# Top-k attention and two MoE layers on one core: the first chunk's first two feature pairs multiplied with three quarters of x before the last quarter is there, and the first queries transposed in other PSUM banks

## The chip, the cores and the metric

The kernel runs on one core of a Trainium2 chip. The metric is the device time of one execution in microseconds (us), lower is better. Engines: PE is TensorE (matmuls, transposes), DVE is VectorE, ACT is ScalarE, POOL is GpSimd, SP is SyncE, which here issues all the DMAs. Every engine takes its instructions in the order that is fixed when the program is built.

## What is computed

```python
def _attn_ref(q, k, v):                       # (4, 8, 576, 64) each, top_k = 32
    scores = scale * np.matmul(q, k.transpose(0, 1, 3, 2))
    kth = np.partition(scores, -top_k, axis=-1)[..., -top_k:-top_k + 1]
    scores = np.where(scores >= kth, scores, -1000000000.0)
    attn = np.exp(scores - np.max(scores, axis=-1, keepdims=True))
    attn = attn / (np.sum(attn, axis=-1, keepdims=True) + 1e-09)
    return np.matmul(attn, v).astype(np.float32)

x = attn_out.transpose(0, 2, 1, 3).reshape(2304, 512)
x = ((1 / (1 + np.exp(-(x @ w_gate)))) * (x @ w_val)) @ w_out     # 512 -> 1536 -> 512
h = np.maximum(x @ w_in, 0.0)                                     # 512 -> 2048
return ((h * h) @ w_out2).astype(np.float32)                      # 2048 -> 512
```

The weights arrive as 64-bit numbers; everything else is 32-bit.

## The kernel before

The 2304 tokens are cut into 18 blocks of 128, and these into chunks: six chunks of one block, then six of two. For each chunk the attention goes through four pairs of heads (`hp` 0 to 3). Such a pair loads its queries and values (`Pair.load`), turns its queries with PE (`queries`, line 341, result `qpt`, copied by ACT to `qt`), makes scores for each head (`scores`, line 381, PSUM tile `sp`, copied by ACT to `S`), finds the 32 largest of each row with four MAX8 and three MATCH_REPLACE8 on DVE (`rank`, lines 392 and 393), applies the threshold and the exponential on ACT (lines 418 and 434), turns the probabilities with PE (`transpose`, lines 482 and 493, tiles `tp` and `tq`) and multiplies with the values (`values`, line 543, tile `xp`). ACT copies `xp` to one quarter of the chunk's x (line 551): head pair hp is quarter hp of the 512 features. In the first chunk the keys are also turned on the way (`prep_keys`, lines 167 to 175: `kpt` on PE, `kp` by ACT, `kl` by DVE).

The first two chunks (`PLAIN`, their x is the tile `x_plain`) go through the MoE in fp32 in `moe32`. Layer 1 has six feature pairs `fp`. A pair (`l1_pair`) is 16 matmuls into one PSUM bank `pg` of the pool `ps_w`: gate and value weights (`wg`, `wv`), two blocks of 128 features each, four quarters of x each (line 932; quarter c is the innermost loop). Then ACT takes the tanh of the gate half (line 941, `th`), POOL and DVE make `g`, and `l1_acc` (line 954) adds eight matmuls with `wo` into `acc`. After six pairs ACT copies `acc` back over x (line 972, "the x2 copy" below), and layer 2 follows (`l2_pair` with `wi` into `ph`, line 979; `l2_acc` with `w2`, line 996). Each fp32 matmul is two records in the trace.

Before that the weights must be made into fp32: blocks of 128 x 512 are fetched as raw 64-bit words (line 591, 512 KB each), and `conv` turns them with two ACT instructions a block (lines 613 and 620), one of DVE a pair of blocks (617) and one of POOL a block (621). `gram_pair` (line 639, tiles `wg_n`, `wv_n`, `wo_n`, ...) sums squares of the weights on PE for the scales of the later fp16 path. There are 68 blocks in the order wg, wv, wo, wi, w2. Chunks 3 to 12 then use weights split in two fp16 parts.

What sets the order: the loop at the end of the kernel calls `weight_step()`, the attention generator `att` and the `moe32` generator `body` by three clocks `tw`, `ta` and `tm`, and `at(t)` gives what it emits the priority t. A list scheduler then orders all instructions of each engine by priority and by its own estimates of when they can run. In this program it had already put single matmuls of `pg_0` and `pg_1` early: one each after the first, the second and the third quarter of x, since the first accumulation needs only `wg` and one quarter at a time. The PSUM pools have two banks each: `ps_t` (tag `tr`: all the transposes `kpt`, `qpt`, `tp`, `tq` and `xp`), `ps_a` (tag `acc`: the sums), `ps_w` (tag `wk`: `pg`, `ph`), and `ps_s` two more for the scores.

Of the kernel before, what the change touches and what calls it, by code (L numbers as in the profile page):

```python
# [10 lines left out]
F32 = mybir.dt.float32  # L11
# [10 lines left out]
P = 128  # L22
# [15 lines left out]
PLAIN = (0, 1)  # L38
# [26 lines left out]
DTURN = 5  # L65
DTAIL = 14
KA = 7
GLATE = 30.0
EARLY = ("wg", "wv")
PB = 10  # L70


TB = 15
# [3 lines left out]
def tile_topk_attention__then__two_moe_layers(  # L77
# [14 lines left out]
    nc = tc.nc  # L92
# [196 lines left out]
    class Pair:  # L289
# [9 lines left out]
        def load(self):  # L299
            ci, hp = self.ci, self.hp  # L300
            for tt in self.tts:
                qn = apool.tile([P, 2, 2, D], F32, tag="qn", bufs=2, name=f"qn_{tt}_{hp}")
                for b, s0, o, n in pieces(tt):
                    for a in range(2):
                        nc.sync.dma_start(
                            qn[o : o + n, :, a, :],
                            q[b, 2 * hp : 2 * hp + 2, s0 : s0 + n].rearrange("h p d -> p h d"),
                        )
                self.qt[tt] = qn
            for b, _, _ in self.segs:  # L310
                if ci >= TCI:
                    t = apool.tile(
                        [P, 2, 2, CB + 1, D], F16, tag="v", bufs=2, name=f"v_{ci}_{hp}_{b}"
                    )
                    nc.sync.dma_start(t, vscr[(b, hp)])
                    self.vt[b] = t
                    continue
                t = apool.tile([P, 2 * CB + 1, D], F32, tag="v", bufs=2, name=f"v_{ci}_{hp}_{b}")
                src = v[b, 2 * hp : 2 * hp + 2]
                for j in range(2):  # L320
                    nc.sync.dma_start(
                        t[:, j * CB : (j + 1) * CB], src[j, 0:SM].rearrange("(p c) d -> p c d", c=CB)
                    )
                    nc.sync.dma_start(t[j * ST : (j + 1) * ST, 2 * CB], src[j, SM:S])
                self.vt[b] = t
# [10 lines left out]
        def queries(self, tts):  # L336
            for tt in tts:
                qn = self.qt[tt]
                pt = ps_t.tile([P, 512], F32, tag="tr", name=f"qpt_{tt}_{self.hp}")
                for j in range(2):  # L340
                    nc.tensor.transpose(  # L341
                        pt[:, j * P : (j + 1) * P], qn[:, j].rearrange("p a d -> p (a d)"), ident
                    )
                p3 = pt[:, 0 : 2 * P].rearrange("p (j t) -> p j t", j=2)
                ps = pieces(tt)
                for b, _, o, n in ps:

                    qt = apool.tile([P, 2, 2, P], F32R, tag="qt", bufs=2, name=f"qt_{tt}_{self.hp}_{b}")
                    for p_b, _, o_, n_ in ps:
                        if p_b != b:  # L350
                            nc.gpsimd.memset(qt.bitcast(F32)[:, :, :, o_ : o_ + n_], 0.0)
                    sl = slice(o, o + n)
                    nc.scalar.copy(qt[:, 0, :, sl], p3[:, :, sl])

                    whole = qn.rearrange("p j a d -> p j (a d)")[:, :, sl]
                    nc.scalar.copy(whole, p3[:, :, sl])
                    nc.gpsimd.tensor_tensor(
                        qt[:, 1, :, sl], whole, qt[:, 0, :, sl], op=ALU.subtract
                    )
                    self.qt[(tt, b)] = qt  # L360
# [108 lines left out]
        def transpose(self, j, i, wk, dg):  # L469
# [4 lines left out]
                    [P, CB, self.N], F32, tag="PT", bufs=3, name=f"PT_{self.ci}_{h}"  # L474
                )
            ptr = self.pt[j]
            tp = ps_t.tile([P, 512], F32, tag="tr", name=f"tp_{tt}_{h}")
            for c in range(CB):
                o, x = tp[:, c * P : (c + 1) * P], wk[:, c * P : (c + 1) * P]
                if self.ci < DIAG:  # L480
# [441 lines left out]
    def moe32(ci, xt):  # L922
# [1 line left out]
        assert N == P  # L924
        accs = []

        def l1_pair(fp):
            pg = ps_w.tile([P, 512], F32, tag="wk", name=f"pg_{ci}_{fp}")
            for t, name in enumerate(("wg", "wv")):
                for e in range(2):  # L930
                    for c in range(KM):
                        nc.tensor.matmul(
                            pg[:, (2 * t + e) * N : (2 * t + e + 1) * N],
                            fblk(name, c, (2 * fp + e) * P, P),
                            xt[:, c, :],
                            start=(t == 0 and e == 0 and c == 0),
                            stop=(c == KM - 1),
                            skip_group_check=True,
                        )
            th = mpool.tile([P, 2 * N], F32, tag="hi", bufs=HIB, name=f"th_{ci}_{fp}")  # L940
            nc.scalar.activation(th, pg[:, 0 : 2 * N], AF.Tanh, scale=0.5)
            nc.gpsimd.tensor_scalar(th, th, 1.0, 0.5, op0=ALU.add, op1=ALU.mult)
# [4 lines left out]
        def l1_acc(fp, g):  # L947
# [3 lines left out]
            for e in range(2):  # L951
                f = 2 * fp + e
                for d in range(KM):
# [6 lines left out]
                        skip_group_check=True,  # L960
                    )

        prev = None
        for fp in range(NF1 // 2):
            g = l1_pair(fp)
# [55 lines left out]

    nchunk = len(chunks)
    done = set()
    xsp = {}

    xts = {}
# [4 lines left out]
    def attention():  # L1031
# [62 lines left out]
        def tail(n, after=None):  # L1094
# [30 lines left out]
            if j == 1 and i == len(pr.tts) - 1:  # L1125
                if pr.ci < TCI:
                    pr.values()
                if pr.hp == NHP - 1:
                    if pr.ci in PLAIN:
                        xsp[pr.ci] = pr.xt  # L1130
# [106 lines left out]
    def at(t):  # L1237
        tc.cur_priority = base + int(t * 50)
# [19 lines left out]
    for ci in PLAIN:  # L1258
        n = 0
        while True:  # L1260
            if nstep[0] == len(steps):
                tw = 1e8
            if body is None and ci in xsp:
                have("wv")
                body = moe32(ci, xsp.pop(ci))
                tm = max(ta, tw if tw < 1e8 else 0)
            if body is not None and tm <= min(tw, ta):
                if n == 1:
# [85 lines left out]
```

## Time and profile before

| | |
|---|---|
| median of 3 runs | 1227.74 us (1220.72 to 2309.37) |
| the profiled execution | 1218.28 us, of which the span from first to last instruction is 1216.2 us |
| busy in the span | PE 1158.1 us, DVE 919.5, POOL 833.4, ACT 802.0 |
| granted TensorE clock, mean of the span | 0.989 |
| DMA | 153.91 MB, 127 GB/s over the span; 350 GB/s and more between 30 and 90 us |

Times in rows are microseconds from the span's start. A timeline row gives the start, the length from the first start to the last end, the instruction, how many of them, and in brackets how long the engine stood idle before it and what released it. The granted clock is the share of full speed that the throttle let PE have in a stretch: its two levels are 1.2 and 2.4 GHz, so 0.50 is a stretch wholly at the lower one. Matmuls overlap: the step from one group's start to the next group's start tells what a group costs.

### The profile page before, as it was taken

How to read it: one execution, taken by the hardware profiler on the slowest of the kernel's cores; microseconds unless marked ns; L12 is line 12 of the kernel's file. 1: busy time of each engine (PE TensorE's matmuls, PEld its weight loads, DVE VectorE, ACT ScalarE, POOL GpSimd, SP SyncE). 2: the span in 40 equal slices, each digit the busy share in tenths (PEclk: the TensorE clock that was granted, in tenths of full speed). 3: DMA queues.
4: the chain of work that ended last, by engine and by line, in shares of the span. 5: the costliest groups of instructions: out<-in, count | busy, mean ns of one | idle time of the engine just before them, and what ended most of it. 6: DMA issues, size and time to landing. Idle time of an engine off the chain costs nothing.

```text
span 1216.2 us, 30575 instructions
## 1 busy us (share of the span) xinstructions
PE 1158.1 (95%) x11477; PEld 941.4 (77%) x11477; DVE 919.5 (76%) x1921; ACT 802.0 (66%) x1695; POOL 833.4 (69%) x1294
## 2 busy tenths in 40 slices
PE   6879999999799799999999999999999999999998
PEld 5659878878679678788787688768876886886875
DVE  5899878899779988999999799999699969010010
ACT  3999985777767777777778667766577666222122
POOL 1698984687875688878879967896597659324223
PEclk9889999999899999999999999999999999999999
DMA  6999963324353477666676666556245513200000
GB/s 153 355 359 320 305 181 105 89 68 133 99 148 104 116 153 156 143 138 135 144 173 136 137 146 130 122 117 145 50 89 126 99 40 63 45 1 1 18 1 18
DMA packets 243187, 153.91 MB, mean 127 GB/s; under 512 B 193120, under 2 KB 209504, under 8 KB 243040
## 3 DMA queue, kind: packets, MB, share of 16 engines
q1 hardware_dynamic: 243040, 151.97, 49.3%
q8 instruction: 90, 1.47, 0.5%
q14 instruction: 57, 0.47, 0.1%
HBM read 105.51 MB, written 18.09 MB: 102 GB/s over the span
## 4 chain that ended last, share of the span: by engine, by line
PE 48%; DVE 2%; DMA 1%; SPq 0%; issue 0%; ACT 0%; POOL 0%; DVEq 0%; POOLq 0%
PE acc L899 10%; PE ph L878 10%; PE acc L813 7%; PE pv L773 7%; PE pg L773 7%; PE sp L381 3%; PE xp L516 3%; DVE mx L392 1%; DVE W L393 1%; PE qpt L341 1%; DMA kn<-in_k_dram 1%; DMA PT<-pp 0%; PE kpt L167 0%; PE x2pq L845 0%; DVE x2s L848 0%
## 5 line engine op out<-in xcount | busy, mean ns | idle before, releaser
L392 DVE MAX8 mx<-W 128x8 f32<-128x576 f32 x432 | 327.7, 759 | 10.9
L393 DVE MATCH_REPLACE8 W<-mx,W 128x576 f32<-128x576 f32 x288 | 213.9, 743 | 0.0
L878 PE MATMUL ph<-x,wi_w 128*128 128x256 f16 (+1 forms) x1920 | 191.8, 252 | 4.4 <-ACT r L887 2.8
L899 PE MATMUL acc<-w_w,rh 128*128 128x512 f16 x768 | 182.2, 379 | 1.6 <-POOL rh L891 1.6
L878 PEld LDWEIGHTS <-wi_w 128*128 128x128 f16 x1920 | 155.9, 98 | 30.7 <-issue 4.7
L773 PE MATMUL pg<-xs,wg_w 128*128 128x256 f16 (+1 forms) x1440 | 145.4, 251 | 1.3 <-ACT th L783 1.3
L773 PE MATMUL pv<-xs,wv_w 128*128 128x256 f16 (+1 forms) x1440 | 142.6, 251 | 2.1 <-DVE x2s L848 1.7
L381 PE MATMUL sp<-kst,qt 128*128 128x288 f32 x608 | 132.9, 328 | 9.4 <-DMA kst<-ks 4.7
L464 POOL TENSOR_TENSOR pp<-S,pp 128x512 f16<-128x512 f32 x192 | 137.1, 736 | 1.9
L773 PEld LDWEIGHTS <-wg_w 128*128 128x128 f16 x1440 | 117.2, 98 | 19.1 <-issue 3.4
L418 ACT ACTIVATE S<-S,mx 128x576 f32<-128x576 f32 x144 | 111.8, 776 | 27.7 <-DVE mx L392 27.3
L813 PEld LDWEIGHTS <-wo_w 128*128 128x128 f16 x1440 | 118.7, 99 | 13.9 <-issue 2.4
L899 PEld LDWEIGHTS <-rh 128*128 128x128 f16 x768 | 72.1, 98 | 73.4 <-POOL rh L891 1.8
L773 PEld LDWEIGHTS <-wv_w 128*128 128x128 f16 x1440 | 117.0, 98 | 15.4 <-issue 2.7
L392 DVE MAX8 mx<-S 128x8 f32<-128x576 f32 x144 | 107.2, 745 | 26.6 <-ACT S L384 26.4
L384 ACT COPY S<-sp 128x576 f32<-128x576 f32 x144 | 91.8, 637 | 50.6 <-PE sp L381 44.9
L785 DVE TENSOR_TENSOR th<-pv,th 128x512 f32<-128x512 f32 (+1 forms) x60 | 34.6, 576 | 119.2 <-PE pv L773 118.5
L462 POOL TENSOR_SCALAR S<-S,bs 128x576 f32<-128x576 f32 x96 | 71.9, 749 | 54.4 <-ACT pp L461 53.7
L393 DVE MATCH_REPLACE8 W<-mx,S 128x576 f32<-128x576 f32 x144 | 106.9, 743 | 0.0
L813 PE MATMUL acc<-gh,wo_w 128*128 128x256 f16 (+1 forms) x1104 | 104.9, 249 | 1.9 <-ACT gh L788 1.9
L381 PEld LDWEIGHTS sp<-kst,qt 128*128 128x128 f32 x608 | 90.2, 191 | 18.9 <-DMA kst<-ks 5.0
L890 POOL TENSOR_TENSOR r<-r 128x512 f32<-128x512 f32 (+1 forms) x80 | 69.5, 871 | 48.5 <-ACT rh L889 47.4
(236 smaller groups left out, 2222.2 us busy)
## 6 DMA issues: line engine op xcount, KB each, us to landing
kst<-ks SPq DMA_DIRECT2D x112, 288.0 KB, 3.1
v<-vd SPq DMA_DIRECT2D x32, 320.0 KB, 3.5
qn<-in_q_dram SPq DMA_DIRECT2D x128, 64.0 KB, 2.5
wi_r<-in_moe_w_in_dram SPq DMA_DIRECT2D x16, 512.0 KB, 6.4
w_r<-in_moe_w_out_dram SPq DMA_DIRECT2D x16, 512.0 KB, 4.9
v<-in_v_dram SPq DMA_DIRECT2D x56, 128.0 KB, 2.4
wg_r<-in_moe_w_gate_dram SPq DMA_DIRECT2D x12, 512.0 KB, 6.1
wv_r<-in_moe_w_val_dram SPq DMA_DIRECT2D x12, 512.0 KB, 7.3
```

Of the source, the lines that this page charges most:

```text
L381: nc.tensor.matmul(sp[:, e, 0:HALF], l, r, start=(x == 0), stop=(x == len(ops) - 1))
L384: nc.scalar.copy(ss.rearrange("p (e s) -> p e s", e=2), sp[:, :, 0:HALF])
L392: return nc.vector.max(m8, st.cur).ins
L393: ins = nc.vector.match_replace(st.wk, m8, st.cur, NEG).ins
L418: nc.scalar.activation(wk, wk, AF.Prelu, bias=kth, scale=-1.0, alpha=1.0 / BIG)
L462: nc.gpsimd.tensor_scalar(wk, wk, rz, 1.0, op0=ALU.mult, op1=ALU.mult)
L464: nc.gpsimd.tensor_tensor(pp[:, o : o + e - f], wk[:, f:e], pp[:, f:e], op=ALU.subtract)
L773: nc.tensor.matmul(pp[:, e * N : (e + 1) * N], wblk(wd, a, c, f0, P), xs[:, b_, c, :], start=(e == 0 and n == 0), stop=(n == 3 * KM - 1), ...
L813: nc.tensor.matmul(accs[d // 2][:, (d % 2) * N : (d % 2 + 1) * N], wblk("wo", a, f, d * P, P), gh[:, b_, e * N : (e + 1) * N], start=(f == ...
L878: nc.tensor.matmul(ph[:, e * N : (e + 1) * N], wblk("wi", a, c, f0, P), x2[:, b_, c, :], start=(e == 0 and n == 0), stop=(n == 3 * KM - 1) ...
L890: nc.gpsimd.tensor_tensor(r, r, r, op=ALU.mult)
L899: nc.tensor.matmul(acc2[i][:, 0:DM], gh[:, b_, e * N + i * P : e * N + (i + 1) * P], wblk("w2", a, f, 0, DM), start=(f == 0 and x == 0), s ...
```

## The change

`products(fp, cs)` is the part of `l1_pair` with the matmuls, for the quarters cs alone. For the first chunk the generator `moe32` now begins by calling it for the pairs 0 and 1 (`FIRST`) with the quarters 0 to 2 (`XC`), and yields; `l1_pair` then adds the last quarter. The driver starts this generator when three head pairs of the chunk are through (`xdone`) and at least eight weight steps are emitted, with the priority of the attention's or the weights' clock. Second, `queries` of the first chunk's first two head pairs (`QACC`) takes its PSUM tile from `ps_a` and no longer from `ps_t`. `SIDEQ` and `TACC` are 0, so the two lines that use them change nothing.

```diff
+SIDEQ = 0
+QACC = 2
+TACC = 0
+FIRST = 2
+FUP = 0
+XC = 3
...
         def queries(self, tts):
             for tt in tts:
                 qn = self.qt[tt]
-                pt = ps_t.tile([P, 512], F32, tag="tr", name=f"qpt_{tt}_{self.hp}")
+                pool, tag = (ps_a, "acc") if self.ci == 0 and self.hp < QACC else (ps_t, "tr")
+                pt = pool.tile([P, 512], F32, tag=tag, name=f"qpt_{tt}_{self.hp}")
...
-        def l1_pair(fp):
-            pg = ps_w.tile([P, 512], F32, tag="wk", name=f"pg_{ci}_{fp}")
+        early = {}
+
+        def products(fp, cs):
+            fresh = fp not in early
+            if fresh:
+                early[fp] = ps_w.tile([P, 512], F32, tag="wk", name=f"pg_{ci}_{fp}")
+            pg = early[fp]
             for t, name in enumerate(("wg", "wv")):
                 for e in range(2):
-                    for c in range(KM):
+                    for c in cs:
                         nc.tensor.matmul(
...
-                            start=(t == 0 and e == 0 and c == 0),
+                            start=(fresh and t == 0 and e == 0 and c == cs[0]),
...
+        def l1_pair(fp):
+            products(fp, range(XC if fp in early else 0, KM))
+            pg = early.pop(fp)
...
+        if ci == PLAIN[0] and FIRST:
+            for fp in range(FIRST):
+                products(fp, range(XC))
+            yield
...
+            if (
+                ci == PLAIN[0]
+                and FIRST
+                and body is None
+                and xdone.get(ci, 0) >= XC
+                and nstep[0] > NF1 // 2 + XC // 2
+            ):
+                body = moe32(ci, xts[ci])
+                at(max(ta, tw) - FUP)
+                next(body)
+                tm = 1e9
-            if body is None and ci in xsp:
+            if ci in xsp and (body is None or tm == 1e9):
                 have("wv")
-                body = moe32(ci, xsp.pop(ci))
+                x = xsp.pop(ci)
+                body = moe32(ci, x) if body is None else body
```

Every engine issues the same instructions as before; only their order changes, on PE over the first 70% of its rows. Line numbers in rows of the changed kernel are larger (932 is 945, 381 is 388, 972 is 993, 591 is 599).

On PE, behind the third quarter of x (`xp_2`, the tile that ACT copies into it), stood before, with `pg_0` and `pg_1` the two feature pairs, `tp_6`, `tq_6` the transposed probabilities of the fourth head pair's first head and `sp_2` the scores of the second chunk's second head pair:

```order
L639 MATMUL wv_n<-wv_c_603 128x128
L932 MATMUL pg_0_1040<-x_plain,wg_c_280 128x128
L932 MATMUL pg_1_1118<-x_plain,wg_c_280 128x128
L482 MATMUL tp_6_909<-dg_6_866,S_6_627 128x128 x4
L381 MATMUL sp_2_971<-kst_2_0_892,qt_1_0_904 128x288
L493 MATMUL tq_6_916<-dg_6_866,S_6_627 64x128
L639 LDWEIGHTS wv_c_681
```

and now stands, from `tp_6` to the last of the scores `sp_2` (its first rows, and its last):

```order
L490 MATMUL tp_6_935<-dg_6_866,S_6_627 128x128 x4
L945 MATMUL pg_0_868<-x_plain,wg_c_280 128x128
L945 MATMUL pg_0_868<-x_plain,wg_c_209 128x128 x2
L945 MATMUL pg_0_868<-x_plain,wg_c_280 128x128
L945 MATMUL pg_0_868<-x_plain,wv_c_524 128x128 x2
L945 MATMUL pg_0_868<-x_plain,wv_c_582 128x128
L945 MATMUL pg_0_868<-x_plain,wv_c_524 128x128 x2
L945 MATMUL pg_0_868<-x_plain,wv_c_582 128x128
L945 MATMUL pg_1_881<-x_plain,wg_c_280 128x128
L388 MATMUL sp_2_997<-kst_2_0_918,qt_1_0_930 128x288
L945 MATMUL pg_1_881<-x_plain,wg_c_209 128x128
```

Behind these come `tq_6`, six more of `pg_1`, the other three of `sp_2`, and the last two of `pg_1`. In all nine matmuls more of each pair stand here, 18 together; behind the last quarter four of each pair are left, where there were 13.

On ACT, the rows up to the first chunk's x2 copy (line 972 before, `x_plain<-acc_0`) were, with `w_c` and `w_r` the blocks of the last weight, `PT` and `PE` copies of transposed probabilities, `S_1` a copy of scores:

```order
L434 ACTIVATE S_0_1754,bs_0_2032<-S_0_1754,bs_0_2032 128x576
L384 COPY S_1_1817<-sp_1_1818 128x576
L485 COPY PT_6_1831<-tp_6_1832 128x512
L494 COPY PE_3_1838<-tq_6_1839 64x128
L613 ACTIVATE w_c_1562<-w_r_0_1536 128x512
L620 ACTIVATE w_r_0_1536<-w_r_0_1536 128x512
L972 COPY x_plain<-acc_0_1208 128x512
```

and are now:

```order
L441 ACTIVATE S_0_1754,bs_0_2032<-S_0_1754,bs_0_2032 128x576
L621 ACTIVATE w_c_1562<-w_r_0_1534 128x512
L628 ACTIVATE w_r_0_1536<-w_r_0_1536 128x512
L993 COPY x_plain<-acc_0_1208 128x512
L493 COPY PT_6_1831<-tp_6_1832 128x512
L502 COPY PE_3_1838<-tq_6_1839 64x128
```

Three copies moved from ahead of the x2 copy to behind it. Counted from the program's start, ACT has the same number of every other instruction ahead of it in both (56 each of lines 613 and 620, 17 each of 418 and 434).

On SP, the first weights (`wg_r`) were issued four at once, ahead of the next chunk's queries `qn_0`, the fourth pair's keys `ks_3` and the loads `kst`:

```order
L591 DMA wg_r_0_197<-in_moe_w_gate_dram 128x1024
L591 DMA wg_r_0_199<-in_moe_w_gate_dram 128x1024
L591 DMA wg_r_0_201<-in_moe_w_gate_dram 128x1024
L591 DMA wg_r_0_203<-in_moe_w_gate_dram 128x1024
L305 DMA qn_0_619<-in_q_dram 128x2x64 x2
L181 DMA ks_3_422<-kp_3_409 64x576 x2
L181 DMA ks_3_422<-kl_3_410 64x576 x2
L333 DMA kst_0_0_717<-ks_0_108 128x576
L333 DMA kst_1_0_820<-ks_0_108 128x576
L591 DMA wg_r_1_205<-in_moe_w_gate_dram 128x1024
```

and are now:

```order
L599 DMA wg_r_0_197<-in_moe_w_gate_dram 128x1024
L599 DMA wg_r_0_199<-in_moe_w_gate_dram 128x1024
L311 DMA qn_0_619<-in_q_dram 128x2x64
L187 DMA ks_3_422<-kp_3_409 64x576 x2
L187 DMA ks_3_422<-kl_3_410 64x576 x2
L311 DMA qn_0_619<-in_q_dram 128x2x64
L339 DMA kst_0_0_717<-ks_0_108 128x576
L339 DMA kst_1_0_820<-ks_0_108 128x576
L599 DMA wg_r_0_201<-in_moe_w_gate_dram 128x1024
L599 DMA wg_r_0_203<-in_moe_w_gate_dram 128x1024
L599 DMA wg_r_1_205<-in_moe_w_gate_dram 128x1024
```

The third and the fourth block went behind these loads; the fifth to the eighth follow directly.

## Rows read from the trace of the kernel before

**Rows 1.** The page, section 1: busy time, share of the span, instructions.
```profile
PE 1158.1 (95%) x11477; PEld 941.4 (77%) x11477; DVE 919.5 (76%) x1921; ACT 802.0 (66%) x1695; POOL 833.4 (69%) x1294
```

**Rows 2.** Windows: stretch, its length, busy (x records) of five engines, clock, DMA share, GB/s.
```profile
80.00:85.00 5.00, 4.63 (x22) 3.78 (x22) 4.79 (x10) 5.00 (x11) 4.84 (x6) 0.50 1.00 339
...
40.00:90.00 50.00, 38.22 (x269) 28.65 (x269) 48.53 (x98) 49.05 (x101) 44.76 (x50) 0.80 1.00 366
90.00:140.00 50.00, 50.00 (x458) 46.10 (x458) 47.10 (x98) 49.25 (x102) 46.14 (x53) 1.00 0.92 315
...
150.00:200.00 50.00, 50.00 (x418) 39.65 (x417) 40.62 (x82) 35.15 (x69) 33.37 (x46) 1.00 0.53 155
200.00:550.00 350.00, 325.90 (x4033) 280.01 (x4033) 309.99 (x659) 257.09 (x582) 258.51 (x442) 0.99 0.50 122
550.00:1050.00 500.00, 496.34 (x4855) 392.72 (x4854) 430.89 (x900) 343.12 (x722) 384.50 (x630) 1.00 0.54 115
```

**Rows 3.** Timeline of ACT, from 80 to 96 us and around the x2 copy.
```profile
80.31 0.62 ACT L384 COPY S<-sp 128x576 f32<-128x576 f32 x1
...
89.49 0.27 ACT L551 COPY x_plain<-xp 128x128 f32<-128x128 f32 x1
...
95.69 0.36 ACT L941 ACTIVATE th<-pg 128x256 f32<-128x256 f32 x1
...
144.23 0.61 ACT L485 COPY PT<-tp 128x512 f32<-128x512 f32 x1
...
144.87 0.69 ACT L613 ACTIVATE w_c<-w_r 128x512 f32<-128x512 f32 x1
...
146.00 0.59 ACT L972 COPY x_plain<-acc 128x512 f32<-128x512 f32 x1
146.47 0.66 ACT L384 COPY S<-sp 128x576 f32<-128x576 f32 x1
147.00 0.71 ACT L613 ACTIVATE w_c<-w_r 128x512 f32<-128x512 f32 x1
```

**Rows 4.** Timeline of PE, from 78 to 147 us.
```profile
78.36 0.66 PE L381 MATMUL sp<-kst,qt 128*128 128x288 f32 x3 [0.71 <-POOL qt L357]
...
82.56 2.02 PE L482 MATMUL tp<-dg,S 128*128 128x128 f32 x8
...
87.18 0.43 PE L543 MATMUL xp<-PE,v 64*64 64x128 f32 x4
...
89.90 1.13 PE L482 MATMUL tp<-dg,S 128*128 128x128 f32 x8 [1.86 <-ACT x_plain L551]
...
120.31 1.95 PE L932 MATMUL pg<-x_plain,wg_c 128*128 128x128 f32 x16
122.10 1.73 PE L932 MATMUL pg<-x_plain,wv_c 128*128 128x128 f32 x14
...
141.53 0.46 PE L482 MATMUL tp<-dg,S 128*128 128x128 f32 x2 [1.04 <-ACT x_plain L551]
...
146.64 5.62 PE L979 MATMUL ph<-x_plain,wi_c 128*128 128x128 f32 x48 [0.47 <-ACT x_plain L972]
```

**Rows 5.** Timelines of PE and of DVE, from 18 to 32 us.
```profile
18.25 1.09 PE L167 MATMUL kpt<-ident,kn 128*128 128x128 f32 x4 [0.85 <-DMA kn<-in_k_dram]
...
22.20 0.66 PE L341 MATMUL qpt<-ident,qn 128*128 128x128 f32 x2 [0.43 <-DMA qn<-in_q_dram]
...
31.61 0.82 DVE L175 TENSOR_TENSOR kl<-kpt,kp 128x512 fp32r<-128x512 f32 x2 [2.21 <-ACT kp L174]
```

**Rows 6.** Timeline of SP's queue and of ACT, and the landing of line 591's DMAs.
```profile
26.83 1.96 SPq L591 DMA_DIRECT2D wg_r<-in_moe_w_gate_dram  x4
...
36.86 0.90 SPq L591 DMA_DIRECT2D wg_r<-in_moe_w_gate_dram  x2
...
39.51 0.69 ACT L620 ACTIVATE wg_r<-wg_r 128x512 int32<-128x512 uint32 x1
...
DMA to landing us min/median/max: 4.6/7.0/10.6
```

More of the change, by code (lines that the diff above doesn't have):

```diff
@@ L304, in load @@
                     for a in range(2):
-                        nc.sync.dma_start(
+                        (nc.scalar if ci == 0 and hp == 0 and a < SIDEQ else nc.sync).dma_start(
                             qn[o : o + n, :, a, :],
@@ L476, in transpose @@
             ptr = self.pt[j]
-            tp = ps_t.tile([P, 512], F32, tag="tr", name=f"tp_{tt}_{h}")
+            pool, tag = (ps_a, "acc") if self.ci == 0 and self.hp < TACC else (ps_t, "tr")
+            tp = pool.tile([P, 512], F32, tag=tag, name=f"tp_{tt}_{h}")
             for c in range(CB):
@@ L1023, in tile_topk_attention__then__two_moe_layers @@
     done = set()
+    xdone = {}
     xsp = {}
@@ L1127, in tail @@
                     pr.values()
+                    xdone[pr.ci] = pr.hp + 1
                 if pr.hp == NHP - 1:
```

## The prediction

> **What bounds the kernel now.** I read the busy times first, then a table of stretches, then the timelines of PE and ACT where the stretches meet. Over the span PE is the full engine: 1158.1 of 1216.2 us [rows 1]. But that is a mean over stages, and the stretches tell them apart [rows 2]. From 40 to 90 us PE is busy 38.22 of 50 us and runs at a mean granted clock of 0.80, while ACT is busy 49.05, DVE 48.53 and the DMA engines all the time, at 366 GB/s: this is the stage in which the weights come in and are converted. From 90 to 140 us PE is busy all 50 us and ACT still 49.25: two engines are full at once. From 150 us on ACT has room (35.15 of 50) and PE alone is full; between 200 and 550 us it stands still for 350.00 − 325.90 = 24.1 us in all, between 550 and 1050 us for only 3.7 us.
>
> So PE work that goes from behind 90 us to ahead of it leaves a full stretch for one with idle time, which is worth its whole length if PE alone sets the pace afterwards. The reader should check that against ACT [rows 3, 4]. The last quarter of x shows how: its products end on PE at 87.6 us, ACT copies them at 89.49 us, in its turn, without having been idle, and PE stands 1.86 us for it. At the other end, ACT makes the x2 copy at 146.00 us, again in its turn, and PE waits for it 0.47 us; a little before, PE waits 1.04 us for another copy of ACT. Layer 2 of the first chunk therefore starts by ACT's order, and PE's backlog is only as long as ACT lets it be.
>
> **The change part by part.**
>
> *The products.* 18 matmuls, 36 records, leave the stretch behind 90 us. Sixteen such records take 122.10 − 120.31 = 1.79 us from start to start, so 0.112 us each at the full clock [rows 4], and 36 make 4.0 us. Ahead of 90 us they lie in idle time: 11.8 us of it between 40 and 90 us [rows 2]. The cover is not complete, since they stand ahead of three of the four score matmuls of the second chunk's second pair; what that may cost is a rival below. The two banks of `ps_w` were held from the first quarter on before too, so nothing else loses a bank.
>
> *What of the 4.0 us reaches layer 2.* PE could come to the x2 copy 4.0 + 1.04 + 0.47 = 5.5 us sooner, if ACT were ready. ACT's queue ahead of that copy loses one copy of scores, 147.00 − 146.47 = 0.53 us, and the two copies of probabilities, 144.87 − 144.23 = 0.64 us [rows 3], and nothing else: 1.17 us. Since ACT is full from 40 us on, the copy comes 1.2 us sooner, and the rest of PE's freed time becomes waiting between 90 and 146 us. The same is seen at the first tanh: PE needs only four matmuls of `pg_0` behind the last quarter now and would be done near 91.5 us, 3.9 us before 95.69, yet ACT's queue brings that tanh some 1.2 us sooner only. The bounds of this part are 0 and −5.5 us; I take −1.2, because ACT's rows have no gap there.
>
> *The queries' banks.* In the first 35 us the transposes of keys, queries and probabilities shared two banks. Now PE does the second pair's scores ahead of the third pair's keys, and does not stand 0.85 us for the third pair's keys nor 0.43 us for its queries [rows 5]. That is 1.28 us on PE, on the way to the fourth pair's keys, for which DVE stands 2.21 us at 31.61. Attention then runs up to 1.28 us sooner into the stage in which ACT is full. Bounds: 0 (if the wait is only pushed to another place in these 35 us) and −1.28; I take −1.3, since DVE's wait is longer than what is taken away.
>
> *The weights' order on SP.* The third and fourth block of `wg` were issued by 28.8 us; now they stand behind the loads of keys, behind which the next block went out at 36.86 us [rows 6], so they go out near 36.86 − 1.28 = 35.6 us. A block needs 4.6 to 10.6 us to land. ACT wants the fourth block at 39.51 us, or 38.2 with the gain above, and the third about as late in the new order. At 4.6 us the block is there at 40.2, at the median of 7.0 at 42.6. What ACT loses is between 0, if its order puts the attention's copies into the gap, and 4 us. I take 0.5 us, near the least landing time, because the queue carries less than before while this block waits; the upper part is a rival.
>
> *The rest.* POOL and DVE do the same work; the moved order of attention behind 150 us is priced at nothing, covered by the 24.1 us in which PE already waits for others there; if that cover is gone it is the fourth rival.
>
> Sum: −1.2 − 1.3 + 0.5 = −2.0 us at the x2 copy. Behind it PE is the full engine, so I let the 2.0 us pass to the end. Against the profiled execution, 1218.28 us, that is 1216.3 us. The other runs shown lie 2.4 and 9.5 us above the profiled one, without the run at 2309.37, so the forecast leans to the low side of what a median may show.
>
> **The rivals.**
>
> *PE passes everything on.* For it speaks that PE is at 50 of 50 from 90 us on, and that both waits on ACT near 141 and 146 us are short; an order in which ACT does the attention's copies sooner could let PE through. Then −5.5 − 1.3 = −6.8 us: 1211.5 us. Against it speaks ACT's 49.25 of 50 in the same stretch. Chance 0.2.
>
> *The products hold up the scores (the other side).* Ahead of the last three score matmuls of `sp_2` now stand 16 matmuls more than before, 32 records, 3.6 us at the full clock. PE stood 0.71 us there before [rows 4]; so the scores end up to 2.9 us later than 79.0. ACT took them at 80.31, 1.3 us behind their end; it would stand 1.6 us, with the weights' conversions behind it in its queue. At the lower clock level, which holds all of 80 to 85 us [rows 2] and at which eight records of `tp` took 2.02 instead of 1.13 us, the 32 records cost 7.2 us and ACT stands 7.2 − 0.71 − 1.3 = 5.2 us. As ACT is full, all of it shows at the x2 copy: 1216.3 + 5.2 = 1221.5 us, slower than before. It decides from the point where the scores end later than ACT reaches their copy by more than the 2.0 us gained. Against it: ACT's new order brings the third quarter's copy ahead of two blocks of conversions, so that the products can start sooner. Chance 0.15.
>
> *The weights are late.* If the stage from 40 to 90 us runs at the pace of the DMAs, then the two blocks that go out later are a hole that isn't filled again: 2 × 524 KB at 366 GB/s [rows 2] are 2.9 us, and the time is 1216.3 − 0.5 + 2.9 = 1218.7 us. For it: the DMA share of 1.00. Against it: ACT has no idle time in front of its conversions there, so it, not the DMAs, sets their pace. The Trainium skill has a rule here that speaks for this rival (DMA: Bandwidth & Descriptors, "Where 436 GB/s comes from"): transfers between HBM and on-chip memory are held by the HBM side at about 358 GB/s for one core. The 366 GB/s of the row are at that figure, so by the rule the stage is bound by DMA; by ACT's own rows, ACT is bound there too. I give it a chance of 0.1.
>
> *The order behind 150 us.* PE's order differs over 70% of its rows, and the 24.1 us of waits between 200 and 550 us are made of many short ones. A third more or less of them is 8 us: 1208 or 1224 us. Nothing in the profile says which. Chance 0.15, half on each side.
>
> **How the numbers follow.** The forecast's own case has 0.4, from 1213 to 1219 us. The rivals reach from 1208 to 1224. Outside that I add what a measurement adds: the runs shown stand up to 9.5 us above the profiled one, so the upper end goes to 1230, and the lower end to 1205, a little under the better half of the last rival. Two per cent, about what a measurement of this kernel can tell from no change, is 24 us; every case above lies within it. Only a sum of good luck in the order and a low measurement reaches below 1203, or of bad luck above 1243: 0.04 and 0.03.
>
> **What would show it right or wrong.** Right: two groups of `pg` records, some 20 and 16, between 70 and 82 us, and only 8 of each pair behind the last quarter; the granted clock from 70 to 90 us no lower than before; ACT still without gaps from 40 to 140 us; PE with waits for ACT between 90 and 146 us, some 3 us more in all than before; the x2 copy near 144 us. Wrong, towards the first rival: the x2 copy near 140 us and no new waits of PE. Wrong, towards the second: an idle ACT in front of a score copy near 80 us. Wrong, towards the third: ACT idle in front of lines 613 or 620, released by a DMA. If the x2 copy moves as said and the end does not, the 2.0 us went into waits between 200 and 550 us.

## The result, and the profile after

The changed kernel takes 1228.08 us (median of 20 runs, 1223.69 to 1232.55) where the kernel before takes 1221.54 on the same chip: ratio 1.0052, 95% interval 1.0038 to 1.0066. It is 0.5% slower, some 6.4 us; 1216.3 and slightly faster was forecast. The profiled execution of the changed kernel is at 1225.55 us, its span 1223.8.

PE's busy time, in the page's first section, has grown by 4.7 us against [rows 1], for the same 11477 matmul records:

```profile
PE 1162.8 (95%) x11477; PEld 947.5 (77%) x11477; DVE 922.2 (75%) x1921; ACT 803.4 (66%) x1695; POOL 830.8 (68%) x1294
```

The windows of the changed kernel stand against [rows 2]; columns as there:

```profile
80.00:85.00 5.00, 3.92 (x42) 3.02 (x42) 4.60 (x11) 4.95 (x11) 4.55 (x7) 1.00 0.98 365
40.00:90.00 50.00, 40.31 (x306) 32.73 (x306) 46.08 (x98) 49.78 (x102) 41.72 (x49) 0.95 1.02 378
90.00:140.00 50.00, 46.80 (x420) 42.36 (x420) 48.13 (x94) 49.24 (x101) 45.52 (x53) 0.99 0.90 315
...
200.00:550.00 350.00, 321.99 (x3946) 277.79 (x3945) 307.82 (x653) 253.58 (x573) 256.60 (x438) 0.97 0.49 121
550.00:1050.00 500.00, 495.41 (x4847) 391.86 (x4846) 434.66 (x906) 345.65 (x726) 383.19 (x630) 1.00 0.54 114
```

Up to 140 us this is what the prediction wanted: 306 PE records from 40 to 90 us where there were 269, and behind 90 us 3.2 us of standing (50 − 46.80) where PE had stood nowhere. Not all of that is for ACT: up to the x2 copy PE waits 3.0 us for ACT where it had waited 1.5, so the sign "some 3 us more" is only half there. The loss begins in the fourth row: PE stands 350.00 − 321.99 = 28.0 us there, not 24.1, and does 3946 records, not 4033. The granted clock of that row is 0.97, not 0.99, but it is not the loss: run e13 below has 0.97 there too and is no slower than the kernel before, and from 450 to 700 us, where most of the loss is counted, the clock is 1.00 in both kernels.

The timeline of ACT in the changed kernel, against [rows 3] and [rows 6]:

```profile
39.65 0.67 ACT L621 ACTIVATE wg_c<-wg_r 128x512 f32<-128x512 f32 x1 [1.62 <-DMA wg_r<-in_moe_w_gate_dram]
...
78.67 0.61 ACT L391 COPY S<-sp 128x576 f32<-128x576 f32 x1
...
87.43 0.27 ACT L559 COPY x_plain<-xp 128x128 f32<-128x128 f32 x1
...
93.41 0.39 ACT L958 ACTIVATE th<-pg 128x256 f32<-128x256 f32 x1
...
144.06 0.58 ACT L993 COPY x_plain<-acc 128x512 f32<-128x512 f32 x1
```

The x2 copy has gone from 146.00 to 144.06, the last quarter's copy from 89.49 to 87.43, the first tanh from 95.69 to 93.41: some 2 us each, as forecast. And PE, against [rows 4]:

```profile
72.24 1.91 PE L945 MATMUL pg<-x_plain,wg_c 128*128 128x128 f32 x8
73.95 1.67 PE L945 MATMUL pg<-x_plain,wv_c 128*128 128x128 f32 x12
...
77.85 0.64 PE L388 MATMUL sp<-kst,qt 128*128 128x288 f32 x3
...
87.75 1.91 PE L490 MATMUL tp<-dg,S 128*128 128x128 f32 x8 [0.86 <-ACT x_plain L559]
89.45 1.06 PE L945 MATMUL pg<-x_plain,wg_c 128*128 128x128 f32 x4
90.30 1.06 PE L945 MATMUL pg<-x_plain,wv_c 128*128 128x128 f32 x4
...
144.69 3.39 PE L1000 MATMUL ph<-x_plain,wi_c 128*128 128x128 f32 x28 [1.14 <-ACT x_plain L993]
```

The early products are there from 72 us on, with only 8 records of each pair behind the last quarter; PE now waits 1.14 us for the x2 copy (0.47 before). Then the lead is lost. Output copies of chunks 1, 3, 5 and the last, on ACT, first of the kernel before:

```profile
282.46 0.56 ACT L1014 COPY ob<-acc 128x512 f32<-128x512 f32 x1
...
448.17 0.69 ACT L917 ACTIVATE ob<-acc,x2s 128x512 f32<-128x512 f32 x1 [0.51 <-PE acc L899]
...
590.77 0.69 ACT L917 ACTIVATE ob<-acc,x2s 128x512 f32<-128x512 f32 x1 [0.53 <-PE acc L899]
...
1211.79 1.40 ACT L917 ACTIVATE ob<-acc,x2s 128x512 f32<-128x512 f32 x2 [6.43 <-PE acc L899]
```

and of the changed kernel:

```profile
277.56 0.56 ACT L1035 COPY ob<-acc 128x512 f32<-128x512 f32 x1
...
449.78 0.70 ACT L925 ACTIVATE ob<-acc,x2s 128x512 f32<-128x512 f32 x1
...
593.74 0.69 ACT L925 ACTIVATE ob<-acc,x2s 128x512 f32<-128x512 f32 x1
...
1219.34 1.40 ACT L925 ACTIVATE ob<-acc,x2s 128x512 f32<-128x512 f32 x2 [6.43 <-PE acc L907]
```

4.9 us ahead at 282 us, 3.0 behind at 591, 7.6 behind at the end. An output copy only says how far one chunk is. What all of PE's work up to a time is worth I count from the groups of matmuls, each at its step from start to start where PE runs through (0.056 us for an fp16 record of 128 columns: 24 of them every 1.35 us). By that PE is some 1 us ahead of before at 150 us, 0.8 behind at 300 and 450, 7 behind at 550, 7 to 8 at 700. This count is an estimate: two profiles of the old order, before and e8, differ in it by some 3 us at 700 us. The windows of the kernel before where most of it goes:

```profile
500.00:550.00 50.00, 50.00 (x677) 41.95 (x676) 48.09 (x100) 35.64 (x80) 38.59 (x71) 1.00 0.65 137
450.00:700.00 250.00, 242.39 (x2881) 200.31 (x2879) 225.85 (x500) 185.00 (x418) 206.62 (x356) 1.00 0.68 145
```

and of the changed kernel:

```profile
500.00:550.00 50.00, 46.31 (x642) 38.32 (x640) 44.16 (x93) 33.13 (x73) 38.02 (x70) 1.00 0.63 131
450.00:700.00 250.00, 235.97 (x2823) 196.10 (x2823) 223.60 (x487) 181.24 (x408) 196.20 (x342) 1.00 0.66 141
```

From 450 to 700 us PE stands 14.0 us (250.00 − 235.97) where it had stood 7.6. Its timeline shows the longest waits in the changed kernel from 500 us on, which the kernel before has not:

```profile
523.53 0.94 PE L524 MATMUL xp<-PT,v 128*64 128x128 f16 x27 [1.48 <-DMA PT<-pp]
...
537.05 0.94 PE L524 MATMUL xp<-PT,v 128*64 128x128 f16 x27 [1.64 <-DMA PT<-pp]
...
619.43 0.76 PE L388 MATMUL sp<-kst,qt 128*128 128x288 f32 x4 [1.07 <-DMA kst<-ks]
...
645.97 0.76 PE L388 MATMUL sp<-kst,qt 128*128 128x288 f32 x4 [1.16 <-DMA kst<-ks]
```

Nothing of the edits is in these stretches. They differ in the order that the scheduler wrote.

### The profile page after: what moved, and what is told of

The parts are those of the page before. It is cut to its first block, busy times and chain, and to the rows that moved or that the text cites. A ratio compares the mean times of both kernels' runs of the same rounds, so it can differ in the third digit from the quotient of the medians.

```text
span 1223.8 us, 30559 instructions
## 1 busy us (share of the span) xinstructions
PE 1162.8 (95%) x11477; PEld 947.5 (77%) x11477; DVE 922.2 (75%) x1921; ACT 803.4 (66%) x1695; POOL 830.8 (68%) x1294
## 5 line engine op out<-in xcount | busy, mean ns | idle before, releaser
L886 PE MATMUL ph<-x,wi_w 128*128 128x256 f16 (+1 forms) x1920 | 194.7, 255 | 5.2 <-ACT x L860 4.8
L886 PEld LDWEIGHTS <-wi_w 128*128 128x128 f16 x1920 | 159.6, 100 | 31.5 <-issue 5.7
L388 PE MATMUL sp<-kst,qt 128*128 128x288 f32 x608 | 129.3, 325 | 7.3 <-DMA kst<-ks 6.9
L468 ACT ACTIVATE pp<-S,bs 128x576 f16<-128x576 f32 x96 | 74.4, 775 | 44.1 <-DVE bs L464 18.9
```

Of the source, the lines that this page charges most:

```text
L388: nc.tensor.matmul(sp[:, e, 0:HALF], l, r, start=(x == 0), stop=(x == len(ops) - 1))
L468: nc.scalar.activation(pp[:, 0:S], wk, AF.Copy, scale=rz)
L886: nc.tensor.matmul(ph[:, e * N : (e + 1) * N], wblk("wi", a, c, f0, P), x2[:, b_, c, :], start=(e == 0 and n == 0), stop=(n == 3 * KM - 1) ...
```

## The experiments

Every ratio is against the kernel before on the same chip; there its median was 1221.3 to 1224.4 us, so 0.1% is 1.2 us. "Old" and "new" order: the kernel before's, the changed kernel's. My theory O: the loss is made by the order that the scheduler wrote behind 280 us. Its rivals: P, the early products cost the time; Q, the queries' banks do; C, a lead collides with what follows, whatever the order.

**Each edit alone, and an order alone (e1 to e4).** The first two are the changed kernel with one constant each:

```diff
-QACC = 2
+QACC = 0     (e1, e18: products alone)

-FIRST = 2
+FIRST = 0    (e2: queries' banks alone)
```

> The changed kernel with QACC = 0: the products go early, the queries' transposes stay in ps_t. Theory O (the loss is made by the order that the scheduler writes behind 280 us, the edits themselves gain): x2 copy on ACT at 144.5 to 145.2 us (before 146.00, both edits 144.06), and the end anywhere from 1212 to 1230 us, not tied to the x2 copy. Theory P (the early products cost the time): end at 1227 to 1229, the loss already seen at the chunk 1 output copy (282.46 before) or in waits on ACT from 70 to 150 us. Theory Q (the queries' banks cost it): 1219 to 1222.

Measured: 0.9967 (0.9953 to 0.9982), 1217.62 us. The products alone make the kernel faster; theory P falls. The x2 copy is at 142.20 us, sooner than expected.

> The changed kernel with FIRST = 0: the queries' transposes in ps_a, the products as before. Theory O: x2 copy at 144.5 to 145.5 us, the end anywhere from 1212 to 1230. Theory P: 1219 to 1222. Theory Q: 1227 to 1229. If P or Q holds, e1 and e2 move by amounts that add up to the +6.5 us of the whole change; by O they need not.

Measured: 1.0016 (0.9997 to 1.0035); x2 copy at 145.94. The parts are −0.33% and +0.16%, together −0.17%, where both edits have +0.52%. They don't add up, which by P or Q they should.

e3 is the kernel before with one number of the emission changed, e4 the changed kernel with another:

```diff
-LEAD = 10
+LEAD = 11    (e3)

-LEAD2 = 14
+LEAD2 = 15   (e4)
```

> The kernel before with LEAD 11 for 10: no work, bank or DMA is added or moved between engines, the attention is only emitted one step further ahead of chunks 2 and 3, so that PE's order is the same up to some 290 us and differs behind. Theory O: x2 copy at 146.0 +- 0.3, and the end moves by 2 to 10 us either way (outside 1219.5 to 1223.5) by the order alone. Theories P and Q, and a theory that the order is harmless: 1221.5 +- 2.

Measured: 1.0057 (1.0036 to 1.0079), with the x2 copy at 147.81, later than expected although PE's order up to 293 us is the old one. An order without any edit costs as much as the whole change. That is the plainest evidence for theory O.

> The changed kernel with LEAD2 15 for 14: the order on PE is that of the changed kernel up to some 450 us and another behind. The x2 copy stays at 144.1 in every theory. Theory O: PE's lead over the kernel before is kept up to 450 us as in the changed kernel (-1 to -2 us), and the 5 us that it loses from 500 to 550 us need not come: end between 1216 and 1224, or elsewhere if another stretch goes wrong. Theories P and Q: the time was lost by the edits, 1227 to 1229.

Measured: 1.0039 (1.0026 to 1.0051), 1226.08 us, between the ranges of O and of P and Q. Another order behind 450 us, and little better: PE 1 to 2 us behind before at 450 us, 8 to 10 at 550.

**Early and late order exchanged (e5 to e8).** A table of instruction numbers is added at the end of the kernel, and these lines at the end of its function. They hold every engine, behind a chosen output copy, to the other kernel's order, with dependencies that fix the order of issue only:

```diff
+    table = memoryview(zlib.decompress(base64.b85decode(TABLE))).cast("I").tolist()
+    traced = {i.name: i for i in nc.cur_bb.bb.instructions}
+    while table:
+        names = [f"I-{n}" for n in table[1 : 1 + table[0]]]
+        table = table[1 + table[0] :]
+        for a, b in zip(names, names[1:]):
+            tc.add_manual_dep(traced[b], a, NOSYNC, reason="order of the other kernel")
```

> The changed kernel, both edits in it, whose five engines are held to the kernel before's order for everything that stands behind the output copy of chunk 1 there (about 282 us); ahead of it the order is the changed kernel's. Theory O: the lead at that copy is kept (277.6 to 278.7 in two profiles of the changed kernel's order against 282.5 and 284.1 in two of the old one's, some 5 us), and with the old order behind it the end is 1217 us, 1214 to 1219. Theory C (being ahead is what collides later, whatever the order): 1221 to 1224. Theories P and Q (the edits cost it): 1226 to 1229.

Measured: 1.0011 (0.9997 to 1.0025), 1223.2 us: in theory C's range, not in O's. Most of the loss is gone with the edits still in, but the lead of 5 us at the output copy isn't kept. In this stretch the copy's lead was partly PE doing chunk 1 first and attention later: counted over all work, PE is some 2 us behind before at 300 us.

> The mirror of e5: the kernel before without any edit, held behind the output copy of chunk 1 to the changed kernel's order. Theory O: slower than both kernels, since it has the late order and not the early gain: 1228 + 5 = 1233, from 1229 to 1236. Theory C: 1221 to 1224. Theories P and Q: 1220 to 1223, since nothing of the edits is in it.

Measured: 1.0047 (1.0032 to 1.0063). No edit in it, and nearly the whole loss: P and Q fall, and C too, which wanted 1224 us at most where 1227.35 was measured. It is not the 1233 us that theory O added up.

> e1 (products alone, QACC = 0) held behind the output copy of chunk 1 to the kernel before's order. e1 came to that copy at 275.9 us, 6.5 to 8.2 us ahead of the old order, and lost 7 us between 587 and 703 us. Theory O: the lead is kept, 1213 to 1216, the fastest of all. Theory C: 1218 to 1222. Theory P: 1222 or more.

Measured: 0.9972 (0.9957 to 0.9988), 1217.18 us, between the ranges of O and C: as e1, so the products' gain does not hang on e1's late order.

> The kernel before once more, for a second profile of the same order: the stretch between two output copies should repeat within 1 us where nothing is disturbed, the x2 copy within 2 us (146.00, and 147.81 in e3, whose order is the same so far). Theory O wants the stretches behind 280 us to differ less between two profiles of one order than between two orders (282.46 to 590.77: 308.3 us here, 312.8 in e3).

A single run: 1216.69 us, x2 copy 145.69, chunk 1's output 282.05, chunk 5's 588.52. From 282 to 591 us the old order took 308.3 and 306.5 us in two profiles, 1.8 us apart; the changed kernel took 316.2. That comparison does not weigh the orders: e5, with the old order behind chunk 1's copy, took 316.0 (278.30 to 594.29), so the stretch tells how early chunk 1's copy came. PE is busy 49.83 of 50 us from 500 to 550, as in the first profile.

**A square of the edits, and the late order a third time (e9 to e12).** The same lines with other tables: e9 is the changed kernel, e10 is e2, e11 is e1, all three with the old order behind chunk 0's output copy; e12 is e1 with the new order behind chunk 1's.

> The changed kernel with both edits, held to the kernel before's order already behind the output copy of chunk 0 (about 195 us; e5 was held from 282 us only and came out at 1223.2). Theory O: e5 lost its lead between 200 and 300 us, where its own order still stood (PE waits 2.8 us for DVE's product th there), so with the old order from 195 us on the lead at 200 us stays: about 1.5 to 3 us, 1218.5 to 1220.5. Theory Q (the queries' banks cost the time themselves, ahead of 195 us): 1223 or more again.

Measured: 0.9990 (0.9978 to 1.0002), in theory O's range.

> e2 (queries' banks alone, FIRST = 0) held to the old order behind the output copy of chunk 0. This is the direct effect of that edit on the first 195 us. The prediction said -1.3 + 0.5 = -0.8, so 1220.7. Theory O, from e2's profile (x2 copy at 145.94, PE's work at 150 us level with before): no gain, 1221 to 1222.5. Theory Q: 1223 to 1226.

Measured: 0.9970 (0.9958 to 0.9983), 1221.17 us on a chip where the kernel before has 1224.36: in the ratio, faster than any theory said.

> e1 (products alone, QACC = 0) held to the old order behind the output copy of chunk 0. The direct effect of the early products on the first 195 us. The prediction said -1.2, so 1220.3. Theory O, from e7 (1217.2) and PE's work at 150 us in e1 and e7 (+2.4 us): 1217 to 1218.5. With e9 and e10 it makes a square of the two edits with one order behind them: if the edits act apart, e9 is e10 + e11 less before.

Measured: 1.0005 (0.9992 to 1.0019): theory O missed. PE is some 3 us ahead of before at 150 us and 1 at 200: from chunk 0's output copy on the old order is not one that fits the new start, and PE stands 1.43 us for DVE's `kn` at 198.84 us. The square neither closes nor fails to: −0.30% and +0.05% make −0.25% against −0.10% for both, and each has an interval of 0.13% each way.

> e1 (products alone) held behind the output copy of chunk 1 to the changed kernel's order. The price of that late order was 5.9 us behind the kernel before's start (e6 less before) and 4.9 us behind both edits (after less e5). Theory O: the same price behind the products, 1217.2 + 5 = 1222 to 1223.5. Theory C (a lead collides by itself): 1217 to 1219, as in e1 and e7.

Measured: 1.0019 (1.0000 to 1.0038), near theory O's range (1222 to 1223.5 against 1221.5 is 1.0004 to 1.0016) and not in C's. Here is what the runs agree on. The new order behind 282 us costs 0.47% behind the old start (e6), 0.41% behind both edits (1.0052 less e5) and 0.47% behind the products alone (e12 less e7): 5.0 to 5.7 us, three times. All of PE's waits from 450 to 700 us together show the same 5 us: 6.1 to 9.5 us in the eight profiles with the old order there (before, e5, e7 to e11, e13), 14.0, 13.6 and 12.4 us in the three with the new one (the changed kernel, e6, e12). The sum is not an exact measure of an order: with orders of their own there, e2 (1.0016) stands 12.5 us and e3 (1.0057) 10.7. The row of e13:

```profile
450.00:700.00 250.00, 242.10 (x2868) 200.44 (x2866) 225.59 (x497) 184.87 (x418) 204.01 (x354) 0.99 0.69 145
```

and of e6:

```profile
450.00:700.00 250.00, 236.44 (x2824) 196.18 (x2822) 224.87 (x490) 183.55 (x414) 198.21 (x345) 1.00 0.64 141
```

The two kinds of waits for DMAs come with the new order too, whatever stands ahead of it. PE's groups of `xp` from 500 to 550 us and of `sp` from 600 to 800 us, with the idle time ahead of them, in e6:

```profile
L516 PE MATMUL xp<-PT,v 128*64 128x128 f16 x106 | 4.3, 220 | 2.7 <-DMA PT<-pp 2.7
...
L381 PE MATMUL sp<-kst,qt 128*128 128x288 f32 x144 | 29.1, 319 | 2.2 <-DMA kst<-ks 2.2
```

in e12:

```profile
L524 PE MATMUL xp<-PT,v 128*64 128x128 f16 x112 | 5.2, 242 | 3.8 <-DMA PT<-pp 3.8
...
L388 PE MATMUL sp<-kst,qt 128*128 128x288 f32 x144 | 29.1, 319 | 3.3 <-DMA kst<-ks 3.1 <-ACT S L391 0.2
```

and in e7, with the old order there:

```profile
L524 PE MATMUL xp<-PT,v 128*64 128x128 f16 x112 | 4.1, 221 | 0.0
...
L388 PE MATMUL sp<-kst,qt 128*128 128x288 f32 x148 | 31.7, 324 | 0.8 <-DMA kst<-ks 0.8
```

They do not tell the orders apart by themselves: with the old order there, e5 and e13 stand 1.4 and 1.0 us for `PT`.

**Where in the late order (e13, e14).** The changed kernel with the same lines, held from later copies.

> The changed kernel held to the kernel before's order behind the output copy of chunk 3 (about 449 us). Theory L (the late loss is made between 450 and 590 us): 4 to 5.5 us less than the changed kernel, so a ratio of 1.0006 to 1.002 against before, like e5 (1.0011). Theory M (it is made between 282 and 450 us, and only shows later): as the changed kernel, 1.004 to 1.006.

Measured: 0.9992 (0.9977 to 1.0007). Just under theory L's range and far from M's: the whole loss is made behind 449 us. With the old order taken up at 196, 282 or 449 us the kernel with both edits stands at 0.9990, 1.0011 and 0.9992.

> The changed kernel held to the kernel before's order only behind the output copy of chunk 5 (about 592 us). Theories L and M: everything is lost by then, 1.004 to 1.006 as the changed kernel. Theory N (the order behind 590 us has its part, 1 us and more): 1.003 or less.

Measured: 1.0028 (1.0013 to 1.0044), theory N. Behind 590 us the new order costs about 0.24% (1.0052 less 1.0028), between 449 and 590 us (e14 less e13) about 0.36%. The interval of such a difference is some 0.2% each way, so the first of the two is barely clear of nothing.

**Are the waits the cause (e15 to e18)?** The changed kernel in its own order, held, with a few of PE's matmuls moved. The table of instruction numbers holds these moves:

| run | matmuls of PE that waited, with their start | put behind the next matmuls |
|---|---|---|
| e15 and e16, on the changed kernel | 27 of `xp` at 523.53 us, 27 of `xp` at 537.05 us | 22, 28 |
| e16, besides | 4 of `sp` at 619.43 us, 4 of `sp` at 645.97 us | 11, 15 |
| e17, on e1 | 27 of `xp` at 489.55 us, 27 of `xp` at 527.02 us, 4 of `sp` at 613.70 us, 6 of `sp` at 723.99 us | 16, 34, 17, 10 |

> The changed kernel in its own order, but on PE the 27 matmuls of xp that waited 1.48 us (523.5 us, xp_7_3) stand behind the next 22 matmuls, and the 27 that waited 1.64 us (537.05 us, xp_8_0) behind the next 28: work that was ready. If these two waits are the late loss or most of it: 3.1 us less than the changed kernel, 1.0025 to 1.003 against before. If they only show a backlog of the attention that another wait would show: 1.0045 to 1.006.

Measured: 1.0039 (1.0020 to 1.0057). That lies between the two ranges and its interval reaches into both, so this run alone decides nothing.

> e15, and the four score matmuls that waited 1.07 us for kst at 619.43 us (sp_10_1) stand behind the next 11 matmuls, the four that waited 1.16 us at 645.97 us (sp_10_3) behind the next 15. If these waits are the loss there: 2.2 us less than e15, a ratio of 1.002 to 1.0025 against before. If the attention is late as a whole, so that a wait moved away comes back elsewhere: 1.0035 to 1.005, as e15.

Measured: 1.0031 (1.0019 to 1.0042). The four waits are gone, and other waits of PE in these stretches have grown. Its timeline:

```profile
528.34 0.44 PE L348 MATMUL qpt<-ident,qn 128*128 128x128 f32 x2 [0.54 <-ACT xf L538]
532.37 1.50 PE L821 MATMUL acc<-gp,wo_w 128*128 128x128 f16 x24 [1.15 <-ACT ob L925]
...
651.90 2.78 PE L781 MATMUL pv<-xs,wv_w 128*128 128x256 f16 x24 [1.34 <-ACT th L791]
...
664.56 0.63 PE L173 MATMUL kpt<-ident,kn 128*128 128x128 f32 x4 [1.46 <-DMA kn<-in_k_dram]
```

In the changed kernel these four places stood 0, 0.53, 0.64 and 0.52 us. Of 1.48 + 1.64 + 1.07 + 1.16 = 5.35 us moved away, 4.49 − 1.69 = 2.8 us come back there, and the time falls by 0.21% = 2.6 us, with an interval of some 2 us each way. The profile shows none of that gain: PE's waits from 450 to 700 us are 14.0 us in all, as in the changed kernel:

```profile
450.00:700.00 250.00, 236.03 (x2820) 195.62 (x2820) 223.91 (x487) 182.82 (x413) 197.25 (x343) 1.00 0.65 141
```

> e1 (products alone, ratio 0.9967) in its own order, but the four groups that waited for a DMA longest behind 480 us stand later: xp_7_2 (1.57 us at 489.55) behind 16 matmuls, xp_8_0 (1.80 us at 527.02) behind 34, sp_10_1 (1.89 us at 613.70) behind 17, sp_13_1 (1.04 us at 723.99) behind 10. If each such wait goes through to the end: 0.9 + 1.8 + 1.9 + 1.0 = 5.6 us less, 0.992. If half comes back elsewhere, as in e15: 0.994 to 0.995. If all comes back: 0.9967.

Measured: 0.9958 (0.9945 to 0.9972).

> e1 once more, on the chip of e17: 0.9967, within 0.9953 and 0.9982.

Measured: 0.9944 (0.9925 to 0.9963), a little below the range expected. e17, whose four waits are gone (0.3 us for `PT`, 0.2 for `kst` left), is no faster than e18 beside it, which has them.

So the waits for the DMAs show where the order is late, but they are at most half of its price; in e1's order they are worth nothing measurable. The price is PE standing some 5 us more from 450 to 700 us, in many short waits together. Which rows of an order make these waits is not settled.

The best version is the changed kernel with `QACC = 0`: 1217.62 and 1219.37 us where the kernel before has 1221.99 and 1224.20, 0.3 to 0.6% faster than it and about 0.9% faster than the change as it was made.

## Why the prediction was wrong

**What bounds the kernel; the x2 copy: right.** Four profiles with the old start have the x2 copy at 145.69 to 147.81 us, mean 146.71; eight with both edits at 143.36 to 147.09, mean 144.60. That is −2.1 us where −2.0 was forecast. Copies of the same order differ by 2 us and more, so single profiles would not have shown it.

**The products: right mechanism, the term's size depends on the order.** −1.2 us came from counting what leaves ACT's queue ahead of the x2 copy. With products alone the copy comes at 142.01 us in the mean of six profiles (141.46 to 142.94), −4.7 us. The built order says why: there 9 instructions leave ACT's queue ahead of the copy, not 3: two copies of queries and four conversions of `w2` besides. In the changed kernel exactly the three leave that I had counted. The copy does follow ACT's order, but "loses ... nothing else" holds for that one order only.

**The queries' banks and the weights' order: the gain came, and the late blocks took it back.** In the first 35 us the waits shrink as forecast (DVE's 2.21 us at 31.61 [rows 5] became 1.15 at 29.14). ACT, the fourth of the busy times, is 2.2 us ahead at 36 us and has lost 2.1 us of that at 45 us, first in the kernel before:

```profile
0.00:36.00 36.00, 26.30 (x96) 20.21 (x98) 21.33 (x45) 15.47 (x33) 4.97 (x16) 1.00 0.70 189
36.00:45.00 9.00, 7.12 (x52) 5.20 (x52) 7.02 (x14) 8.75 (x19) 5.46 (x7) 1.00 0.90 290
```

and in the changed kernel:

```profile
0.00:36.00 36.00, 28.14 (x110) 21.53 (x110) 22.80 (x49) 17.71 (x38) 5.31 (x18) 1.00 0.68 175
36.00:45.00 9.00, 8.56 (x41) 6.52 (x40) 7.89 (x16) 6.63 (x14) 5.33 (x7) 1.00 0.99 375
```

What it stands for is a block of `wg`: 1.62 us at 39.65 us, 0.8 to 2.8 us in the ten profiles with this edit, inside the bounds of 0 and 4 us but more than the 0.5 us taken. With the queries' edit alone no instruction on ACT leaves the queue ahead of the x2 copy, and the copy comes at 145.94 and 146.90 us in two profiles: −0.3 us where the two terms together had −0.8. So the sum of −2.0 us came out by luck in its parts: the products alone moved the copy by −4.7 us, the queries' edit alone by −0.3, both together by −2.1.

**Letting the 2.0 us pass to the end: not shown.** With the old order behind it the change is at −0.10% (e9), +0.11% (e5) and −0.08% (e13); the forecast was −0.16%. Two of the intervals hold it, e5's does not, and all three hold zero. What the following order does with a lead is as large as the lead: e10 has next to none at its x2 copy (146.90 us) and ends 0.30% sooner.

**The rest, "priced at nothing, covered by the 24.1 us": the step that failed.** The order behind 282 us costs 5.0 to 5.7 us. PE's waits between 200 and 550 us did not cover it, they grew by 3.9 us, and from 450 to 700 us they grew from 7.6 to 14.0 us; a part of the price, by e14 some 3 us and barely clear of nothing, lies behind 590 us, where I had looked for none. Idle time of a full engine that is made of many short waits is no cover: each is the place where this order just fits, and another order has others. It was the fourth rival, whose slow half (1224 us) I gave 0.075. Its size was about right, since 1224 against the profiled 1218.28 us is +0.47% where +0.52% was measured; most of the 4 us that are missing to 1228 are the base (below). It should have been the largest chance, since over 70% of PE's rows moved.

**The other rivals.** The first (PE passes everything on) is not the changed kernel, but the x2 copies of e1 come near it (−4.7 of −5.5 us). The second is not seen: the last three score matmuls of `sp_2` end at 78.5 us (77.85 + 0.64), not later than the 79.0 of before, ACT copies these scores at 78.67 us without having stood, and PE's clock from 80 to 85 us is 1.00, not 0.50 as in [rows 2]; the work that filled the stretch came ahead of it, and whether that raised the clock was not tried by itself. The third's sign is there, ACT idle for 1.62 us in front of line 613 (621 now) for a DMA, but not as a bound of the stage: from 40 to 90 us ACT was busy 49.78 of 50 us, and the DMAs, all of them loads of weights, queries, values and keys from HBM, moved 378 GB/s. The Trainium skill's rule of about 358 GB/s for one core (DMA: Bandwidth & Descriptors, "Where 436 GB/s comes from") does not agree with that row, so here the measurement decides.

**The base.** The forecast started from the profiled 1218.28 us, which lies 3.3 us under the median of 20 runs, and so leaned low by as much.

## What to carry to other kernels

Where a scheduler writes the order, price the rows it moves far behind an edit: here an order alone was worth 0.4 to 0.6%, more than both edits together. Test it by a change that does no work (one emission number), and take the edit's own effect with the old order held behind it; an edit that is slower as built may be faster with one half left out. A wait that you can name is not yet a cause: move it away, see whether the time falls or the next wait grows, and weigh an order by all waits of a stretch together.

## What the runs showed of the hardware

Two executions of one order differ early. From 40 to 90 us the granted clock was 0.76 to 0.80 in four profiles with the old start and 0.86 to 0.97 in eight with both edits, and the x2 copy moved by up to 3.7 us within one order (143.36 to 147.09). The kernel before's median was 1221.3 us on one chip and 1224.4 on another. The DMAs that turn `pp` to `PT` took 3.2 to 5.7 us to land from 505 to 540 us in the changed kernel, and PE stood 1.48 and 1.64 us for two of them.
